# Last K/V chunk taken into the common loops of a one-core decode kernel, with a later wait in the loop and other small moves

## The chip, the cores and the metric

The kernel runs on one core of one Trainium2 chip. Times are microseconds (us) of device time for one execution. "us" in a result is the whole execution; the span of a trace, from first to last instruction, is some 2 us shorter. Engines: TensorE (PE in the profile; PEld is its weight load), VectorE (DVE), ScalarE (ACT), GpSimd (POOL), SyncE (SP). SP issues the large loads; "SPq" in a timeline is such an issue.

## The reference, cut to what matters

One query token, 16 query heads over 8 K/V heads, 65536 cached positions, head width 256, and a small MLP beside it. Nearly all the work is reading the caches once: 2 x 8 x 65536 x 256 bf16 values, 537 MB.

```python
q = (x @ wq).reshape(B, Sq, Hq, Dh).transpose(0, 2, 1, 3)
k, v = jnp.repeat(k_cache, 2, axis=1), jnp.repeat(v_cache, 2, axis=1)
scores = jnp.einsum("bhqd,bhkd->bhqk", q, k) * (Dh ** -0.5)
o = jnp.einsum("bhqk,bhkd->bhqd", softmax(scores), v)
a = o.transpose(0, 2, 1, 3).reshape(B, Sq, Hq * Dh) @ wo
b = token_mlp(layernorm(x), w1, b1, w2, b2)        # 448 x 1792, elementwise
return g * a + (1 - g) * b                         # g = sigmoid(sum(x * gate_w))
```

## The kernel before

Each K/V head's cache is cut into six chunks of 6, 6, 5, 5, 5 and 5 blocks of 2048 positions: 48 chunks in all. There are two K buffers and one V buffer, and three buffers `kT` for transposed blocks. SP issues the loads in one order, each behind a semaphore that VectorE raises:

```python
def load_k(i):                          # two K buffers
    if i >= 2: sp.wait_ge(s_vf, i - 1)
    sp.dma_start(out=kbuf[i % 2][:, 0:n], in_=kv_src(A_k_cache, i)).then_inc(s_k[i % 2], 16)
def load_v(i):                          # one V buffer
    if i >= 1: sp.wait_ge(s_vf, i + 1)  # s_vf: +1 for each drained P*V
    sp.dma_start(out=vbuf[:, 0:n], in_=kv_src(A_v_cache, i)).then_inc(s_v, 16)
# order on SP: wq (two loads), K0, K1, [projection done] V0, wo, K2, then V1, K3, V2, K4, ...
```

For each chunk VectorE transposes the K blocks into `kT`, TensorE scores each, and P·V of the chunk *before* is put between them:

```python
plan = [(0, 1), (1, 2), (2, 0), (3, 1), (5, 2), (4, 0)]   # (block, kT buffer)
def turns(i):                                             # VectorE
    take(dve, s_k[i % 2], 16)                             # K chunk landed
    for t, (s, b) in enumerate(blocks(i)):
        if t >= 3:                                        # its kT buffer must be free
            take(dve, s_s, 6 - steps[i] + 1 if t == steps[i] - 1 else 1)
        dve.transpose(out=kT[b], in_=kn[block s]).then_inc(s_kt, 1)
    # ... then, in the same chunk: wait for P*V of the chunk before, drain it (s_vf), wait for exp,
    #     transpose P for the next P*V
def scores(s, b, first, last):                            # TensorE: 8 matmuls on kT[b]
    ...
    if last:     ins.then_inc(s_sc, 1)
    elif s < 3:  ins.then_inc(s_s, 1)                     # blocks 0, 1, 2 free a kT buffer
```

On TensorE a loop ran 47 of the 48 turns: score blocks 0 to 3, P·V of the chunk before, the remaining score blocks. The 48th was written out after the loop: all five score blocks, then P·V of chunk 46, then the P·V of the last V, which arrives in four pieces, and the output projection.

The softmax here doesn't subtract the row's maximum and nothing guards it: scores larger than these inputs give would overflow.

## Time and profile before

| | before |
|---|---|
| median of four runs | 1266.46 us (1266.18 to 1266.92) |
| span of the trace | 1264.1 us |
| bytes read | 544.22 MB |
| busy PE / DVE | 57% / 53% |
| transfers, middle of the run | 433 GB/s |

The page of the kernel before: busy shares, then the share of the transfer engines and what they moved in 40 equal slices of 31.6 us.

```profile
PE 721.0 (57%) x4296; PEld 282.0 (22%) x4296; DVE 666.8 (53%) x471; ACT 50.1 (4%) x127; POOL 76.7 (6%) x98
...
DMA  9999999999999999999999999999999999999998
GB/s 407 424 439 430 437 438 425 438 434 428 440 437 423 434 436 433 440 430 435 434 429 435 430 435 440 430 429 437 430 440 435 430 431 435 427 443 435 424 435 350
```

No compute engine is near full; the transfers are, in every slice. The kernel is bound by bytes.

The start of the timeline before: start, duration, engine, line, operation, and in brackets the idle time before it.

```profile
31.50 13.28 DVE L528 STREAM_TRANSPOSE kT<-kbuf 128x2048 f32<-128x2048 f32 x6 [5.82 <-DVEq L520]
...
47.70 0.71 DVE L575 STREAM_TRANSPOSE pT<-p_t 128x512 bf16<-128x512 bf16 x1 [2.38 <-DVEq L520]
48.33 13.23 DVE L528 STREAM_TRANSPOSE kT<-kbuf 128x2048 f32<-128x2048 f32 x6
...
62.41 0.69 DVE L538 COPY og<-pv 128x512 f32<-128x512 f32 x1 [0.84 <-DVEq L520]
63.13 0.33 SPq L247 DMA_DIRECT2D vbuf<-in_A_v_cache_dram  x1
...
70.52 8.89 DVE L528 STREAM_TRANSPOSE kT<-kbuf 128x2048 f32<-128x2048 f32 x4 [3.11 <-DVEq L520]
```

VectorE begins its first transpose at 31.50 us, after 5.82 us of idle.

```profile
L241 SPq DMA_DIRECT2D kbuf<-in_A_k_cache_dram x1: 432/432/432, 1.9 to 1.9; - x1
...
DMA to landing us min/median/max: 25.0/25.0/25.0
```

In this document the time of that first transpose is called T0. The six transposes of chunks 0 and 1 run without a gap. After chunk 0 VectorE goes straight on to chunk 1, because K1 has already landed. At 62.41 the first P·V is drained and 0.72 us later SP issues the second V load (V1). At 70.52 VectorE takes up K2, the load that stands before V1 in the queue; it landed at 70.39.

The same stretch late in the run:

```profile
1201.46 0.69 DVE L539 TENSOR_TENSOR og<-pv,og 128x512 f32<-128x512 f32 x1 [1.86 <-DVEq L520]
1202.18 0.33 SPq L247 DMA_DIRECT2D vbuf<-in_A_v_cache_dram  x1
...
1211.07 2.31 DVE L528 STREAM_TRANSPOSE kT<-kbuf 128x2048 f32<-128x2048 f32 x1 [6.34 <-DVEq L520]
```

Here the V load is issued 8.9 us before the K load ahead of it lands.

And the tail before:

```profile
1247.83 1.91 PE L661 MATMUL sc<-kT,qw 128*128 128x512 bf16 x8 [0.87 <-PEq L657]
1249.66 2.33 PE L675 MATMUL pv<-vbuf,pT 128*4 128x512 bf16 x40
...
1253.32 1.25 PE L771 MATMUL pv<-kbuf,pT 128*4 128x512 bf16 x20 [0.17 <-DMA kbuf<-in_A_v_cache_dram]
...
1258.84 1.43 PE L782 MATMUL misc<-pT,kbuf 128*128 128x2 bf16 x48 [0.56 <-DMA kbuf<-in_A_v_cache_dram]
...
1261.11 0.28 DVE L823 CAST res<-acc 97x112 bf16<-97x112 f32 x1 [0.65 <-PE acc L816]
```

### The profile page before, as it was taken

The page shows a single profiled execution, that of the slowest core. Times are in us where ns is not written, and L with a number is a line of the kernel's source. Part 1 is how long each engine was busy: PE and PEld are TensorE (multiplying, and loading weights), DVE is VectorE, ACT ScalarE, POOL GpSimd, SP SyncE. Part 2 cuts the span into 40 slices and gives each one's busy share as a digit, 9 for nine tenths or more (in the row PEclk, how much of TensorE's full clock was granted, in tenths as well). Part 3 has the DMA queues.
Part 4 walks back from the last instruction along what each step waited for, and adds up shares of the span by engine and source line. Part 5 has one row for each costly group of instructions (what it writes and reads, how often), then busy time and mean ns, then how long its engine had stood idle before and what let it go on. Part 6 is the DMA issues. An engine that isn't in the chain of part 4 may idle for free. (4 is left out here: it accounts for less than half of the span.)

```text
span 1264.1 us, 10739 instructions
## 1 busy us (share of the span) xinstructions
PE 721.0 (57%) x4296; PEld 282.0 (22%) x4296; DVE 666.8 (53%) x471; ACT 50.1 (4%) x127; POOL 76.7 (6%) x98
## 2 busy tenths in 40 slices
PE   3755655456555665556554564566645755456556
PEld 1321222122221222212221221222212222122212
DVE  4845555365544645455555554465545654466444
ACT  0000000000000000000000000000000000000000
POOL 0001010110101101001011011000000000000000
PEclk9876788778777787777887788777877787778887
DMA  9999999999999999999999999999999999999998
GB/s 407 424 439 430 437 438 425 438 434 428 440 437 423 434 436 433 440 430 435 434 429 435 430 435 440 430 429 437 430 440 435 430 431 435 427 443 435 424 435 350
DMA packets 16842, 544.32 MB, mean 431 GB/s; under 512 B 1856, under 2 KB 3906, under 8 KB 4162
## 3 DMA queue, kind: packets, MB, share of 16 engines
q1 hardware_dynamic: 16744, 544.22, 99.7%
q8 instruction: 3, 0.05, 0.0%
q14 instruction: 5, 0.04, 0.0%
q10 hardware_dynamic: 90, 0.01, 0.0%
HBM read 544.22 MB, written 0.00 MB: 431 GB/s over the span
## 5 line engine op out<-in xcount | busy, mean ns | idle before, releaser
L661 PE MATMUL sc<-kT,qw 128*128 128x512 bf16 x2048 | 564.5, 438 | 458.6 <-PEq L657 458.6
L528 DVE STREAM_TRANSPOSE kT<-kbuf 128x2048 f32<-128x2048 f32 x256 | 571.1, 2283 | 310.7 <-DVEq L520 310.7
L661 PEld LDWEIGHTS sc<-kT,qw 128*128 128x128 bf16 x2048 | 213.7, 108 | 807.7 <-issue 644.1
L675 PE MATMUL pv<-vbuf,pT 128*4 128x512 bf16 x2008 | 130.5, 412 | 54.6 <-PEq L709 54.2
L539 DVE TENSOR_TENSOR og<-pv,og 128x512 f32<-128x512 f32 x39 | 27.0, 692 | 108.8 <-DVEq L520 106.3
L675 PEld LDWEIGHTS pv<-vbuf,pT 128*4 128x4 bf16 x2008 | 50.6, 92 | 132.4 <-issue 92.9
L608 ACT ACTIVATE p_t<-sc 128x512 bf16<-128x512 f32 x48 | 28.7, 597 | 1190.0 <-PE sc L661 1190.0
L585 DVE STREAM_TRANSPOSE pT<-p_t 128x512 bf16<-128x512 bf16 x32 | 22.8, 711 | 74.3 <-DVEq L520 74.3
L635 POOL TENSOR_SCALAR t_b<-t_b 128x448 f32<-128x448 f32 x14 | 7.9, 566 | 359.9 <-ACT t_b L617 359.9
L639 POOL TENSOR_SCALAR t_b<-t_b,hw 128x448 f32<-128x448 f32 x14 | 9.0, 640 | 333.4 <-ACT t_b L625 333.4
L538 DVE COPY og<-pv 128x512 f32<-128x512 f32 x8 | 5.5, 692 | 35.4 <-DVEq L520 35.4
L575 DVE STREAM_TRANSPOSE pT<-p_t 128x512 bf16<-128x512 bf16 x8 | 5.7, 711 | 26.9 <-DVEq L520 26.9
L644 POOL TENSOR_TENSOR ymix<-ymix,t_b 128x448 f32<-128x448 f32 x14 | 16.1, 1149 | 1.1
L643 POOL TENSOR_TENSOR t_b<-t_b,u_b 128x448 f32<-128x448 f32 x14 | 15.8, 1128 | 1.2
L638 POOL TENSOR_TENSOR t_b<-t_b,u_b 128x448 f32<-128x448 f32 x14 | 15.8, 1127 | 1.2
L731 PE MATMUL acc<-wo,oT 128*1 128x448 bf16 x28 | 7.0, 374 | 12.7 <-PEq L728 12.7
L591 DVE STREAM_TRANSPOSE pT<-p_t 128x512 bf16<-128x512 bf16 x7 | 5.0, 711 | 13.1 <-DVEq L520 13.1
L617 ACT ACTIVATE t_b<-h_bc,b1T,w1T 128x448 f32<-128x448 f32 x14 | 10.5, 747 | 0.0
L631 POOL TENSOR_SCALAR u_b<-h_bc,w1T,b1T 128x448 f32<-128x448 f32 x14 | 10.0, 718 | 4.1 <-DVE pat L430 2.7
L608 ACT ACTIVATION_READ_ACCUMULATOR p_t<-sc 128x1 f32 x48 | 9.3, 194 | 0.0
L685 PEld LDWEIGHTS misc<-mask,og 128*128 128x128 f32 x64 | 8.7, 196 | 2.3 <-DVE og L539 1.3
L448 PE MATMUL sc<-vbuf,xw 128*128 128x512 bf16 x32 | 9.0, 449 | 0.0
(89 smaller groups left out, 70.3 us busy)
## 6 DMA issues: line engine op xcount, KB each, us to landing
kbuf<-in_A_k_cache_dram SPq DMA_DIRECT2D x32, 5120.0 KB, 33.2
vbuf<-in_A_v_cache_dram SPq DMA_DIRECT2D x31, 5120.0 KB, 20.8
kbuf<-in_A_k_cache_dram SPq DMA_DIRECT2D x16, 6144.0 KB, 36.1
vbuf<-in_A_v_cache_dram SPq DMA_DIRECT2D x16, 6144.0 KB, 24.2
wo<-in_A_wo_dram SPq DMA_DIRECT2D x7, 448.0 KB, 22.3
vbuf<-in_A_wq_dram SPq DMA_DIRECT2D x1, 3072.0 KB, 10.2
kbuf<-in_A_v_cache_dram SPq DMA_DIRECT2D x1, 2560.0 KB, 26.5
kbuf<-in_A_v_cache_dram SPq DMA_DIRECT2D x1, 1280.0 KB, 31.1
```

Source lines behind the costliest of these rows:

```text
L448: last = e.matmul(q_ps[:], lhsT=xw[:, k, HKV - 1 - n:HKV - 1 - n + 128], rhs=rhs, start=(n == 0 and k == 0), stop=(n == HKV - 1 and k >= K ...
L528: dve.transpose(out=kT[b][:].bitcast(FP32), in_=kn[:, s * SB * 128:(s + 1) * SB * 128]).then_inc(s_kt, 1)
L539: return dve.tensor_tensor(out=og[:], in0=pv[:], in1=og[:], op=ALU.add)
L585: dve.transpose(out=pT_t[0][:], in_=p_t[:]).then_inc(s_pt, 1)
L608: ins = act.activation(out=p_t[:], in_=sc[:], func=ACT.Exp, scale=scale, accum_out=den[:, c:c + 1])
L617: ins = act.activation(out=t_b[:], in_=h_bc[:], func=ACT.Square, scale=w1T[:, b:b + 1], bias=b1T[:, b:b + 1],)
L631: lambda: pool.tensor_scalar(out=u_b[:], in0=h_bc[:], scalar1=w1T[:, b:b + 1], scalar2=b1T[:, b:b + 1], op0=ALU.mult, op1=ALU.add,),
L638: lambda: pool.tensor_tensor(out=t_b[:], in0=t_b[:], in1=u_b[:], op=ALU.mult),
L643: lambda: pool.tensor_tensor(out=t_b[:], in0=t_b[:], in1=u_b[:], op=ALU.mult),
L644: lambda: pool.tensor_tensor(out=ymix[:], in0=ymix[:], in1=t_b[:], op=ALU.add),
L661: ins = pe.matmul(sc[:], lhsT=qw[:, q, at:at + 128], rhs=kv[:, :, q // 2, :, q % 2], start=(first and q == 0), stop=(last and q == 7), ski ...
L675: ins = pe.matmul(pv[32 * a:32 * a + 4, :], lhsT=pT[:, k, :, ROW0 + s], rhs=vt[:, j * DH:(j + 2) * DH], start=first and k < 4, stop=last a ...
```

## The change

The intent is one loop for all 48 chunks on both engines, with fewer registers and semaphore steps, and a shorter prologue on VectorE. It has five parts:

1. TensorE and VectorE loops run 48 turns; the last P·V of chunk 46 now stands before the last score block; drains, den sums and the row matmuls of the tail move.
2. In the loop, score block 0 no longer raises the semaphore. The fourth transpose, which overwrites the buffer of block 0, now waits for score block **1**.
3. The small loads on the ACT queue are split by rows or parts: nine loads, not six.
4. The ten mask-row memsets and three other memsets go from VectorE to GpSimd.
5. The multiplies that write the next head's query columns (`queries`) go behind the den sums on VectorE.

```diff
@@ VectorE, turns(i)
-                if t >= 3:
-                    take(dve, s_s, 6 - steps[i] + 1 if t == steps[i] - 1 else 1)
+                if t in (3, steps[i] - 1):
+                    take(dve, s_s)
@@ TensorE, scores()
-            elif s < 3:
+            elif s in (1, 2):
                 ins.then_inc(s_s, 1)
@@ small loads
-        do.dma("act", x_row[:], A_x[0], writes=["x_row"])
-        do.dma("act", gw_row[:], gate_w.rearrange("(o n) -> o n", o=1), writes=["gw_row"])
-        for k, src in enumerate((B_w1[0, :], B_b1, B_w2[:, 0])):
-            do.dma("act", wrow[:, k, :], src.rearrange("(b p) -> b p", p=128), writes=[f"wrow{k}"])
+        for t, src, key, parts in ((x_row, A_x[0, 0], "x_row", 8), (gw_row, gate_w, "gw_row", 7)):
+            do.dma("act", t[...in parts], src[...in parts], writes=[key])        # cut
+        for k, (src, cut) in enumerate(((B_w1[0, :], 9), (B_b1, 2), (B_w2[:, 0], 3))):
+            for lo, hi in ((0, cut), (cut, NF)):
+                do.dma("act", wrow[lo:hi, k, :], src[128 * lo:128 * hi]..., writes=[f"wrow{k}{lo}"])
@@ TensorE loop
-        with nc.Fori(0, total - 1, 1, engines=[PE], head_slot={PE: 0}):
+        with nc.Fori(0, total, 1, engines=[PE], head_slot={PE: 0}):
             for s, b in plan[0:4]:
                 scores(s, b, s == 0, False)
-            with pe.If_lt(f_reg, 1):
+            with pe.If_lt(v_reg, PER):
                 ... P*V of the chunk before ...
             with pe.If_lt(c_reg, big):
                 scores(5, 2, False, False)
             scores(4, 0, False, True)
@@ after the loop
-        for t, (s, b) in enumerate(blocks(last_i)):
-            scores(s, b, t == 0, t == steps[-1] - 1)
-        ... P*V of chunk 46, den sums ...
+        # (both now in the loops; row matmuls moved behind the last V matmuls)
```

## The prediction

> **What bounds it now.** The transfers. The page's slices show DMA at 9 tenths in nearly all 40, and 423 to 443 GB/s in all but the first (407) and the last (350). 544.3 MB at the 433 to 434 GB/s of the middle windows take about 1255 us of the 1264.1 us span; the rest is the wait for first data and the tail. PE is busy 57%, DVE 53%. The Trainium skill ("DMA: Bandwidth & Descriptors", "Where 436 GB/s comes from") gives a ceiling of 435 GB/s; this trace agrees, so no instruction order can speed up the middle. The chain of waits has the last V load for 31.1 us, then 48 small PE matmuls (1.44 us), oT 0.17, output matmuls 0.57, cast 0.28.
>
> **Slack in the middle.** In the timeline a V load is issued at 1202.2 us, 0.7 us after its drain began; the K load queued before it lands only at 1211.1. So 9 us of transfers are still queued: compute that ends 1 or 2 us later empties nothing.
>
> **What the change does.**
> - Prologue: DVE loses the ten row memsets (1.24 us together) and three others (0.57); GpSimd gets them. ACT issues 9 small loads, not 6, at 0.2 to 0.5 us each. The one-element load landed at 10.9 us though issued at 3.0; with more pieces ahead it should land 1 to 4 us later, and the projection (12.9 to 21.7 us) with it. DVE idles 5.8 us until K lands at 31.5, and the first V is wanted only near 40 us. Absorbed.
> - Loop: the fourth transpose waits for the second score block, not the first. With TensorE at its low clock (430 ns a matmul, 3.4 us a block) it starts about 1.5 to 2 us later; scores, P·V and drain perhaps 1 us later. Absorbed by 9 us.
> - Last chunk: before, five score blocks (to 1249.7), then 40 P·V matmuls (2.33 us). After, P·V stands before the last score block (1.92 us), so the last transpose ends about 1253.3 to 1254, not 1251.3. The first piece of last V lands about 1253.3 and its 20 matmuls take 1.25 us; the next lands at 1255.7, the last at 1258.8. The lateness, under 1 us, is caught up there, as are one more drain (0.69) and the den sums (about 1 us).
> - True tail: the four row matmuls (0.37 us) now follow the last V matmuls, beside the oT multiply (0.24 us with its wait): +0.1 to +0.2 us.
>
> **Critical path.** Bytes, large loads and their order are unchanged. Sum: +0.2 us in the tail, 0 to 0.5 us if shadows are tighter than I read, minus at most 0.5 us if the small loads happen to even out the engines' finishing times.
>
> **Prediction:** 1266.8 us, 8 in 10 between 1265.4 and 1268.2. Faster by over 2%: 0.01; within 2%: 0.98; slower by over 2%: 0.01.
>
> **What would show it.** DMA 9 throughout, 544.3 MB; the chain again the last V piece, then the 48 matmuls; DVE busy about 1 us lower; GpSimd 1.5 to 2 us higher; a gap before the fourth transpose where there was none; P·V of the chunk before last ahead of the last score block; the last 20-matmul piece within 1 us of before.
>
> **What would make it wrong.** Loads issued so late that the queue runs dry at each chunk (48 times a microsecond would be 4%): windows with DMA below 0.97. A prologue late by over 9 us. The last V matmuls held by a late transpose (starting after 1259 us). A changed transfer rate from another cause, which the GB/s row would show.

## The result, and the profile after

Four runs took 1267.25 to 1269.83 us, median 1267.95, against 1266.46 before: 1.5 us or 0.1% longer, where 0.2 us had been forecast. The ratio to before is 1.0014, 95% interval 0.9996 to 1.0031. Ratios here are the mean time of one kernel's fast runs over that of the other's of the same rounds, so they are not quite the ratio of the medians quoted.

An interval that wide does not establish 0.1% alone. The traces do, because they show where the time went. The unchanged kernel has long executions too: 4 of its 29 runs took 1267.1 to 1267.95 us. Of the 21 runs of kernels with the later wait in the first two chunks, 19 took over 1267.

The page after, the same lines:

```profile
PE 719.3 (57%) x4296; PEld 276.0 (22%) x4296; DVE 675.2 (53%) x462; ACT 50.1 (4%) x127; POOL 78.7 (6%) x111
...
DMA  9999999999999999999999999999999999999998
GB/s 409 420 408 435 439 436 425 437 435 431 434 436 430 432 441 433 428 434 435 435 439 433 429 435 433 429 437 431 432 441 434 428 433 435 430 439 436 428 433 342
```

The DMA row is unchanged to the digit: a tenth is too coarse here. The GB/s row has one odd number, the third: 408, where before has 439. That slice is 63 to 95 us. The same place in short windows, first before, then after (columns: window, length, busy time and count of PE, PEld, DVE, ACT and POOL, granted clock, DMA share, GB/s; a packet counts whole in the window in which it starts, so a share can exceed 1):

```profile
63.00:66.00 3.00, 2.84 (x14) 1.06 (x11) 0.10 (x1) 0.13 (x1) 0.00 (x0) 1.00 1.01 437
66.00:69.00 3.00, 0.00 (x0) 0.00 (x0) 0.71 (x1) 0.56 (x2) 0.00 (x0) 0.82 1.10 475
69.00:72.00 3.00, 0.00 (x0) 0.00 (x0) 1.48 (x1) 0.00 (x0) 0.00 (x0) 0.50 1.06 459
```

```profile
63.00:66.00 3.00, 3.00 (x32) 1.23 (x36) 3.00 (x2) 0.00 (x0) 0.00 (x0) 1.00 1.01 437
66.00:69.00 3.00, 3.00 (x39) 1.18 (x28) 1.90 (x2) 0.00 (x0) 0.00 (x0) 1.00 0.57 246
69.00:72.00 3.00, 2.15 (x10) 0.77 (x8) 0.00 (x0) 0.69 (x2) 0.00 (x0) 1.00 1.13 377
```

From 66 to 69 us the transfer engines are busy 57%. Summing the packets of the trace from 66 to 80 us gives 6.07 MB before and 5.25 MB after. The 0.82 MB missing are 1.9 us at 433.9 GB/s, the mean of before in that stretch. I call such a loss, counted from 66 to 80 us, the *dip* below. From 100 to 1200 us both traces average 433.5 GB/s: nothing is lost there and nothing won back. The two spans differ by 2.5 us. With each packet spread over its duration, the trace after is 0.04 us of bytes behind at 66 us, 1.94 at 80 us and 1.96 at 1250 us: all of the lost bytes lie in those 14 us. The rest comes at the very end, where the last piece of V lands 1.7 us after the piece before it (below).

The timeline after, for the same events as shown of before:

```profile
33.40 6.70 DVE L539 STREAM_TRANSPOSE kT<-kbuf 128x2048 f32<-128x2048 f32 x3 [6.28 <-DVEq L531]
...
41.26 6.70 DVE L539 STREAM_TRANSPOSE kT<-kbuf 128x2048 f32<-128x2048 f32 x3 [1.16 <-DVEq L531]
...
51.52 6.66 DVE L539 STREAM_TRANSPOSE kT<-kbuf 128x2048 f32<-128x2048 f32 x3
...
60.50 6.70 DVE L539 STREAM_TRANSPOSE kT<-kbuf 128x2048 f32<-128x2048 f32 x3 [2.33 <-DVEq L531]
...
67.72 0.69 DVE L549 COPY og<-pv 128x512 f32<-128x512 f32 x1 [0.52 <-DVEq L531]
68.44 0.33 SPq L248 DMA_DIRECT2D vbuf<-in_A_v_cache_dram  x1
...
72.66 6.66 DVE L539 STREAM_TRANSPOSE kT<-kbuf 128x2048 f32<-128x2048 f32 x3
```

The six transposes have fallen into three and three, with a gap before the fourth: 1.16 us in chunk 0, 2.33 us in chunk 1. V1 is issued at 68.44 us, 5.3 us later than before. Of that, 1.9 us were already there at T0 (33.40 against 31.50, though K0 had landed at 27.1 us), and 3.4 us come from the two chunks: from T0 to V1 it takes 35.0 us, not 31.6. At 72.66 VectorE no longer waits for K2.

The tail after:

```profile
1249.74 2.33 PE L682 MATMUL pv<-vbuf,pT 128*4 128x512 bf16 x40
1252.01 1.92 PE L668 MATMUL sc<-kT,qw 128*128 128x512 bf16 x8
...
1255.66 1.25 PE L747 MATMUL pv<-kbuf,pT 128*4 128x512 bf16 x20 [0.89 <-PEq L531]
...
1260.51 1.21 PE L758 MATMUL misc<-pT,kbuf 128*128 128x2 bf16 x40 [0.56 <-DMA kbuf<-in_A_v_cache_dram]
...
1262.24 0.37 PE L758 MATMUL misc<-pT,kbuf 128*128 128x2 bf16 x8 [0.53 <-DMA kbuf<-in_A_v_cache_dram]
...
1263.64 0.28 DVE L813 CAST res<-acc 97x112 bf16<-97x112 f32 x1 [0.82 <-PE acc L806]
```

P·V of chunk 46 now stands before the last score block. The 20 matmuls on the first piece of the last V start 0.7 us after it landed (1254.94), but at the next pieces PE is idle and waiting when they land, so the new order is in the shadow of that load, as in the kernel before.

### The profile page after: what moved, and what is told of

The parts are those of the page before. It is cut to its first block, busy times and chain, and to the rows that moved or that the text cites. A ratio compares the mean times of both kernels' runs of the same rounds, so it can differ in the third digit from the quotient of the medians.

```text
span 1266.6 us, 10628 instructions
## 1 busy us (share of the span) xinstructions
PE 719.3 (57%) x4296; PEld 276.0 (22%) x4296; DVE 675.2 (53%) x462; ACT 50.1 (4%) x127; POOL 78.7 (6%) x111
## 5 line engine op out<-in xcount | busy, mean ns | idle before, releaser
L668 PE MATMUL sc<-kT,qw 128*128 128x512 bf16 x2048 | 571.4, 437 | 490.2 <-PEq L664 490.2
L668 PEld LDWEIGHTS sc<-kT,qw 128*128 128x128 bf16 x2048 | 210.7, 108 | 849.9 <-issue 696.4
L682 PE MATMUL pv<-vbuf,pT 128*4 128x512 bf16 x2008 | 119.9, 387 | 26.0 <-PEq L712 25.9
L682 PEld LDWEIGHTS pv<-vbuf,pT 128*4 128x4 bf16 x2008 | 47.0, 88 | 95.9 <-issue 50.0
L586 DVE STREAM_TRANSPOSE pT<-p_t 128x512 bf16<-128x512 bf16 x8 | 5.7, 711 | 26.9 <-DVEq L531 26.9
## 6 DMA issues: line engine op xcount, KB each, us to landing
kbuf<-in_A_v_cache_dram SPq DMA_DIRECT2D x1, 2560.0 KB, 25.6
```

Of the source, the lines that this page charges most:

```text
L668: ins = pe.matmul(sc[:], lhsT=qw[:, q, at:at + 128], rhs=kv[:, :, q // 2, :, q % 2], start=(first and q == 0), stop=(last and q == 7), ski ...
L682: ins = pe.matmul(pv[32 * a:32 * a + 4, :], lhsT=pT[:, k, :, ROW0 + s], rhs=vt[:, j * DH:(j + 2) * DH], start=first and k < 4, stop=last a ...
```

## The experiments

Theory A: the later wait of the fourth transpose delays the first drain so far that the queue runs dry before V1 is issued. Theory B: the split small loads make one transfer engine late, and with it the first K chunk and the end. Theory C: the tail, or chance. Rival D: the later wait costs a little at every chunk. The edits are named by what they undo in the diff above. Where an expectation says that the first K lands, read T0.

The traces of e5 to e8 that are kept are of other executions than those described under e5 to e8, whose packets can't be summed again.

### e1: the later wait undone

```diff
  (changed kernel)
-                if t in (3, steps[i] - 1): take(dve, s_s)
+                if t >= 3: take(dve, s_s, 6 - steps[i] + 1 if t == steps[i] - 1 else 1)
-            elif s in (1, 2):
+            elif s < 3:
```

> The changed kernel with one thing undone: the fourth transpose waits for the first score block again, as before. Theory A (the second V load is issued too late and the transfer queue runs dry at 66 to 72 us): the second V load, issued at 68.4 us in the changed kernel and at 63.1 before, comes back to about 65.0 (3.4 us earlier: 1.3 from chunk 0 and 2.1 from chunk 1); the GB/s of 66 to 69 us goes from 246 to above 420; the time falls by 1.3 to 1.9 us against the changed kernel, to a ratio of 1.0000 to 1.0003 to before. Theory B (the split small loads make one transfer engine late, and it stays late to the end): nothing is gained at the end, the ratio stays 1.001 to 1.0015. Theory C (the tail, or chance): also 1.001 to 1.0015, with the dip filled and another loss in its place or none.

Measured: 1266.05 us (1265.95 to 1267.47, five runs), ratio 0.9997 (0.9983 to 1.0010). T0 was 33.39, V1 came at 65.92 us, the dip was 0.61 us. Its window of 66 to 72 us:

```profile
66.00:72.00 6.00, 2.63 (x13) 0.96 (x10) 2.19 (x2) 0.69 (x2) 0.00 (x0) 0.95 0.99 393
```

The loss is gone from the time though the small loads stay split and T0 is late: against B and C. The GB/s did not come back as fully as expected, because V1 was 0.9 us later than I had forecast; the clock, taken up after the table, accounts for that.

### e2: the old small loads

```diff
  (changed kernel)
-  nine split loads on ACT
+  the six loads of before
```

> The changed kernel with the six small loads of before (six, not nine, on ACT). Theory A: the first K chunk lands at 31.5 us again instead of 33.4, so the second V load is issued about 66.5 us, just where the queue ends: most of the dip is gone, ratio 1.0001 to 1.0006. Theory B: the late engine is gone, ratio about 1.0000 to 1.0003, and the last two pieces of V land within 0.5 us of each other (1.7 us apart in the changed kernel). If the first K chunk still lands after 33 us, the small loads did not make it late.

Measured: 1268.34 us (1266.89 to 1268.73), ratio 1.0008 (0.9995 to 1.0022). T0 was 33.53 us all the same, V1 came at 68.63, dip 2.09 us. A miss for what I expected under A, whose numbers rested on T0 coming back to 31.5; and B fails here, since without the split loads T0 is late and the loss is whole.

### e3: both undone

```diff
  (changed kernel)
   the edits of e1 and of e2 together
```

> The changed kernel with both the early wait of the fourth transpose and the small loads of before: only the merged loops, the moved tail and the mask rows on GpSimd are left. Theories A and B: as before within 0.3 us, ratio 0.9997 to 1.0003, second V load at 63 to 63.5 us. Theory C (the tail costs it): ratio 1.0005 to 1.0015.

Measured: 1266.18 us (1266.12 to 1266.35), ratio 0.9996 (0.9982 to 1.0009). T0 31.55, V1 at 64.69 (later than expected), dip 0.02 us. Its last V landed at 1258.88 us, within 0.04 of before, and the final cast began 0.21 us later than before (1261.32 against 1261.11). That is the tail's cost: about 0.2 us, against C. The merged loops and the mask rows on GpSimd cost nothing that can be seen in the time.

### e4: only the later wait, in the kernel before

```diff
  (kernel before)
-                if t >= 3: take(dve, s_s, 6 - steps[i] + 1 if t == steps[i] - 1 else 1)
+                if t in (3, steps[i] - 1): take(dve, s_s)
-            elif s < 3:
+            elif s in (1, 2):
```

> The kernel before with only the later wait of the fourth transpose added. Theory A: second V load at about 66.5 us (63.1 plus 3.4), at the end of the queue; a small dip in the GB/s of 66 to 69 us; ratio 1.0000 to 1.0005. If the wait costs at every chunk (a rival that the windows of the changed kernel speak against), the ratio is above 1.001.

Measured: 1268.42 us (1267.96 to 1269.01), ratio 1.0014 (1.0001 to 1.0028): the whole loss, from this part alone, in the kernel before. T0 33.19, V1 at 67.83, dip 1.42 us:

```profile
66.00:72.00 6.00, 4.54 (x36) 1.66 (x26) 1.87 (x3) 0.69 (x2) 0.00 (x0) 1.00 0.99 369
```

The size is above my figure for A. By that expectation it would have spoken for D, so D had to be tested by itself.

### e7 and e8: the later wait by chunk

Both start from e1, where TensorE raises the semaphore three times in each chunk. The wait is later only where `late` holds:

```diff
-                if t >= 3: take(dve, s_s, 6 - steps[i] + 1 if t == steps[i] - 1 else 1)
+                late = i >= 2          # e7;  e8: i < 2   (i: chunk within the group of six)
+                if t >= 3:
+                    if late:
+                        if t == 3: take(dve, s_s, 2)
+                        elif t == steps[i] - 1: take(dve, s_s)
+                    else: take(dve, s_s, 6 - steps[i] + 1 if t == steps[i] - 1 else 1)
```

> The changed kernel, but in the first two chunks of each group of six the fourth transpose waits for the first score block only (as before); in the other four chunks, 32 of the 48, it keeps the later wait. Theory A (only the first drain has no queue behind it, so only the delay of chunks 0 and 1 costs): second V load at 64.7 to 66 us, no 246 in the GB/s row of 66 to 69 us, time as the run with the early wait everywhere, 1266.0 to 1266.5, ratio 0.9995 to 1.0003. Rival D (the later wait costs a little at every chunk): two thirds of the loss stays, ratio 1.0008 to 1.0012.

> The opposite: the later wait only in the first two chunks of each group of six, the early one in the other 32. Theory A: the whole loss, 1267.3 to 1268.5, ratio 1.0008 to 1.0016, dip of the GB/s at 66 to 72 us. Rival D: a third of the loss, ratio 1.0003 to 1.0006, no dip.

Measured, e7: 1266.46 us (1265.83 to 1267.88), ratio 1.0002 (0.9988 to 1.0015), V1 at 65.12, dip 0.11. e8: 1268.60 us (1266.68 to 1268.71), ratio 1.0011 (0.9997 to 1.0024), V1 at 68.10, dip 1.58. First e7, then e8:

```profile
66.00:72.00 6.00, 1.83 (x9) 0.60 (x7) 2.08 (x2) 0.69 (x2) 0.00 (x0) 0.82 1.02 434
```

```profile
66.00:72.00 6.00, 4.81 (x40) 1.81 (x32) 1.87 (x3) 0.69 (x2) 0.00 (x0) 1.00 0.92 344
```

Thirty-two late waits cost nothing; the sixteen others, of which two lie before V1, cost all of it. D would have it the other way round. The ratios alone overlap; the dip and the medians do not. The kept trace of e7 is one of its long executions (span 1266.9 us, V1 at 66.15, dip 1.11), though its chunks 0 and 1 run without a gap; the clock was late there (below). It speaks no more for D: its bytes are 1.16 us behind those of before at 80 us and 1.15 at 1200.

### e5 and e6: the small loads by themselves

e5 is the kernel before with the nine split loads of the change (its diff above). e6 is the kernel before with six more one-row loads on ACT:

```diff
         do.dma("act", b2_row[:], ...)
+        for n in range(6):
+            do.dma("act", spare[:, n, :], B_b1[128 * n:128 * n + 128]..., writes=[f"spare{n}"])
```

> The kernel before with nothing but the nine split small loads. After the run with the old loads put back (first K landed at 33.5 us there too) I expect them to cost nothing: first V late by about 1 us, first K at 31.5 or about 33.4 us by chance, second V at 63 to 66 us, time as before, ratio 0.9997 to 1.0004. Theory B (split loads make one engine late): first K after 33 us and ratio above 1.0008.

> The kernel before with six more one-row loads on the ACT queue into a tile nobody reads. Theory B': every small load adds a fixed delay to one and the same engine, so the first K chunk, which needs all sixteen, lands 2 us later or more (after 33.5 us), and the second V load moves with it. Chance: first K at 31.5 or about 33.4 us as in the runs so far, ratio 0.9997 to 1.0005.

Measured, e5: 1266.77 us (1266.21 to 1267.92), ratio 1.0004 (0.9990 to 1.0017), T0 33.52, V1 at 65.87, dip 0.69. e6: 1266.42 us (1266.31 to 1267.61), ratio 1.0001 (0.9986 to 1.0017), T0 31.60, V1 at 63.20, no dip. The Trainium skill ("DMA: Bandwidth & Descriptors", "Why a DMA increments its semaphore by 16 and not by 1") says that a load which uses fewer than sixteen transfer engines goes to the lowest-numbered of them. That was the ground of theory B. The trace does not name the engine of a packet, but in all eighteen kept traces, with split, old or added loads, K0 itself landed at 26.6 to 27.2 us: no small load made it late, and B' is refuted.

### e9 to e12: where the two times of T0 come from

e9: kernel before, only the three row loads split. e10: kernel before, only the two one-row loads split. e11: kernel before, unchanged. e12: e5 again.

```diff
  e9 (kernel before)
-        for k, src in enumerate((B_w1[0, :], B_b1, B_w2[:, 0])): one load each
+        for k, (src, cut) in enumerate(((B_w1[0, :], 9), (B_b1, 2), (B_w2[:, 0], 3))): two loads each
  e10 (kernel before)
-        do.dma("act", x_row[:], ...); do.dma("act", gw_row[:], ...)
+        the same two loads, written as 8 and 7 parts
```

> The kernel before with only the three row loads split (six loads, 9 and 5, 2 and 12, 3 and 11 rows). So far the first K chunk landed late (33.4 to 33.5 us) in 5 of 5 traces with the nine split loads and in 2 of 5 without them. If the split of the rows is the cause: after 33.3 us. If chance: 31.5 or 33.4. Time as before within 0.1%.

> The kernel before with only the two one-row loads split in 8 and 7 parts. If spreading these is the cause of the late first K: after 33.3 us; if the rows are, or chance: 31.5 at least as often. Time as before within 0.1%.

> The kernel before, unchanged, for one more trace. If the landing of the first K is chance: 31.5 or 33.4 us, with the second V load at 63.1 or 65.0 us, and in the second case still no more than 0.2 us lost at 66 to 72 us.

> The kernel before with the nine split loads, once more. If these make the first K late: after 33.3 us a sixth time. If chance: 31.5 us is as likely.

Measured, with two runs each: e9 1267.17 us, T0 33.32, V1 64.96, dip 0.05. e10 1267.24 us, T0 33.42, V1 66.68, dip 1.13. e11 1266.27 us, T0 33.37, V1 64.77, dip 0.00. e12 1266.19 us, T0 33.12, V1 64.70, dip 0.01. The unchanged kernel can have its T0 late too, and pays nothing for it: V1 is still in time. e10 has the early wait and a dip all the same: there the two chunks took 33.3 us from T0 to V1, not 31.4 as in e11. The windows of chunk 1 show the granted clock (the number before the last two) lower for longer, first e10, then e11:

```profile
54.00:57.00 3.00, 3.00 (x8) 1.04 (x7) 3.00 (x2) 0.00 (x0) 0.00 (x0) 0.50 0.89 366
57.00:60.00 3.00, 3.00 (x11) 1.20 (x10) 2.94 (x3) 0.00 (x0) 0.00 (x0) 0.70 1.04 448
```

```profile
54.00:57.00 3.00, 3.00 (x12) 1.13 (x11) 3.00 (x3) 0.00 (x0) 0.00 (x0) 0.74 0.89 366
57.00:60.00 3.00, 3.00 (x16) 1.31 (x14) 3.00 (x2) 0.00 (x0) 0.00 (x0) 1.00 1.04 448
```

The first 32 score matmuls of chunk 1 took 9.82 us in e10 and 8.57 in e11, and P·V and the drain came later with them.

### e13 to e16: one trace more of four kernels

e13: the changed kernel. e14: e2. e15: the kernel before. e16: e5.

> The changed kernel once more, one trace. Dose: whatever the landing of the first K chunk L is (31.5 or 33.4 us so far), the second V load comes at L plus 35.0 us, and what the queue loses at 66 to 76 us is about 0.57 us for each us after 65.0: about 0.9 us for L = 31.5, about 1.9 us for L = 33.4.

> The changed kernel with the old small loads, once more. So far the old loads had the first K at 31.5 in 3 of 6 traces and at 33.2 to 33.5 in the other 3; loads with a split had it at 33.1 to 33.5 in 8 of 8. Chance with the old loads: either. Dose as for the changed kernel.

> The kernel before, once more: first K at 31.5 or 33.4 us; second V load 31.5 us after it; loss at 66 to 76 us under 0.1 us either way.

> The kernel before with the split loads, once more: first K after 33 us again if the split makes it late, 31.5 possible if it is chance. Second V load 31.5 to 32.5 us after it; loss under 0.7 us.

Measured (single runs): e13 1268.50 us, T0 33.47, V1 67.92, dip 1.54. e14 1268.28 us, T0 33.33, V1 68.45, dip 1.94. e15 1266.30 us, T0 31.50, V1 63.13, dip 0.00. e16 1266.17 us, T0 33.16, V1 64.79, dip 0.01. e13 tested the dose. V1 came 0.5 us earlier than the expected 35.0 us after T0; for that V1, 0.57 us per us after 65.0 gives 1.66, near the 1.54 measured.

### All traces in one table

Ordered by the issue of V1. The dip is from the packet sums; the GB/s are those of 66 to 72 us; us is the profiled run.

| trace | wait of 4th transpose | small loads | T0 | V1 issued | dip, us | GB/s | us |
|---|---|---|---|---|---|---|---|
| before | early | old | 31.50 | 63.13 | 0.00 | 467 | 1266.30 |
| e15 | early | old | 31.50 | 63.13 | 0.00 | 442 | 1266.30 |
| e6 | early | old + 6 | 31.60 | 63.20 | 0.00 | 459 | 1266.48 |
| e3 | early | old | 31.55 | 64.69 | 0.02 | 475 | 1266.13 |
| e12 | early | split | 33.12 | 64.70 | 0.01 | 475 | 1265.96 |
| e11 | early | old | 33.37 | 64.77 | 0.00 | 467 | 1266.33 |
| e16 | early | split | 33.16 | 64.79 | 0.01 | 457 | 1266.17 |
| e9 | early | rows split | 33.32 | 64.96 | 0.05 | 467 | 1266.35 |
| e7 | early in chunks 0, 1 | split | 33.49 | 65.12 | 0.11 | 434 | 1266.21 |
| e5 | early | split | 33.52 | 65.87 | 0.69 | 377 | 1266.77 |
| e1 | early | split | 33.39 | 65.92 | 0.61 | 393 | 1266.71 |
| e10 | early | x split | 33.42 | 66.68 | 1.13 | 385 | 1268.17 |
| e4 | late | old | 33.19 | 67.83 | 1.42 | 369 | 1268.30 |
| e13 | late | split | 33.47 | 67.92 | 1.54 | 352 | 1268.50 |
| e8 | late in chunks 0, 1 | split | 33.47 | 68.10 | 1.58 | 344 | 1268.60 |
| after | late | split | 33.40 | 68.44 | 1.90 | 311 | 1268.43 |
| e14 | late | old | 33.33 | 68.45 | 1.94 | 287 | 1268.28 |
| e2 | late | old | 33.53 | 68.63 | 2.09 | 279 | 1268.73 |

Up to 65.0 us at most 0.05 us is lost; after that about 0.55 us for each us. Every trace of the table lies within about 0.2 us of this line, whichever edit made V1 late. The six traces with the late wait in chunks 0 and 1 need 34.5 to 35.1 us from T0 to V1, the twelve others 31.4 to 33.3. The kept traces of e5 to e8 have T0 33.45, 33.42, 33.76 and 33.32, V1 at 65.08, 64.82, 66.15 and 68.32, and dips of 0.33, 0.00, 1.11 and 2.05 us: up to 0.5 us above the line.

The dip is a mean over the sixteen transfer engines, and the span can grow by more. In e10 and in the kept trace of e7 two or three engines stand idle for about 2 us after 68 us while the rest work on; the dips are 1.1 us, the spans 1.9 and 2.8 us longer than that of before.

**The clock.** In the kept traces with the early wait in chunks 0 and 1, V1 comes 31.4 to 31.6 us after T0 where the full clock of chunk 1 is granted 22.1 to 23.5 us after T0 (eight traces), and 32.4 to 33.3 us where it is granted 24.2 to 25.4 us after it (e1, e3, e7, e10). This delay, of up to 1.9 us, does not come from the later wait, which these chunks don't have. With a late T0 it goes with a dip, as in e10. It may be what makes some executions of the unchanged kernel long; that is not shown, as none of those has a trace.

**What ends the idle before T0.** The same in all eighteen kept traces: VectorE executes a branch that ends at 25.6 to 27.9 us, then nothing, not even a register instruction (the trace has these, the views leave them out), until 0.2 us before T0, though K0 lands at 26.6 to 27.2. Among the packets in between is one of the kind "instruction", of 8 KB. It starts at 29.5 us where the branch ended by 26.0 (before, e3, e15), and at 31.1 to 31.7 us where it ended at 26.5 or later (the fifteen others); T0 follows its start by 2.0 to 2.1 us each time. My reading is that VectorE stands still for its next instructions, whose fetch waits among the large loads; this is argued, not tested, as the trace doesn't name the engine that a fetch is for. The two times of T0 go with how early the projection is done. In all 22 traces T0 is 31.5 to 31.6 where V0 was issued by 22.01 us, and 33.1 to 33.8 where it was issued at 22.41 or later.

The experiments point to no version that beats both: e1, e3 and e7 are all the same as before within their intervals. With the queue full the bytes set the time.

## Why the prediction was right or wrong, point by point

- **Bound by bytes, middle unaffected: right.** 433.5 GB/s from 100 to 1200 us in both traces. The Trainium skill's ceiling of 435 GB/s ("DMA: Bandwidth & Descriptors", "Where 436 GB/s comes from") agrees with it.
- **"Absorbed by 9 us" (the loop): wrong, and this is the step that failed.** It had three errors, all in one direction.
  1. The slack was read late in the run (8.9 us) and taken for the whole. At V1 the same reading of the kernel before gives 70.52 - 63.13 = 7.4 us.
  2. The landing of the load ahead is not the moment at which the queue runs dry. The table shows the loss starting at 65.0 us, 5.5 us before that landing. Part of this shows in the packets of the trace after: fourteen of the sixteen engines are done with K2 at 67.9 to 69.0 us, up to 2.5 us before it has landed whole, and V1's first packet starts 0.96 us after its issue. The other 2 us or so are not explained. So 1.9 us were usable before V1, not 9.
  3. The delay was set at "perhaps 1 us". In the steady state that is about the size, since each chunk waits for its own K (5.3 us of idle before it in the trace after at 1212 us) and the delay of one chunk does not reach the next. In chunks 0 and 1 it adds up: K1 has already landed when chunk 0 ends, so 1.16 and 2.33 us make 3.5. To this came a T0 that was 1.9 us later.
- **The sum: 0.2 us forecast, 1.5 us measured.** The missing term is the dip, 1.9 us in the trace after (1.5 in its second trace), which the forecast had as 0. It did name the mechanism among what would make it wrong, a queue that runs dry, but looked for it at every chunk rather than once.
- **The fourth transpose starts later: right**, with its reason. The Trainium skill ("TensorE: Matmul & The Clock Gate", "Part 1: The HAM clock gate") says that TensorE's clock is halved after an idle stretch. The trace agrees: weight loads of the first scores of chunk 0 stand 0.43 us apart, and a warm block of eight matmuls takes 1.90 us, 0.24 us each. Two cold blocks would take about 6.9 us, and the first begins only when the first transpose is done, 2.4 us in; three transposes take 6.70 us. So a wait for the second block bites exactly here. The gap was 1.16 us and not 2.6 in chunk 0, because the clock was granted in full from about 39.1 us on.
- **Prologue "absorbed": wrong, by a misread wait.** The one-element load was used at 11.76, not 10.86 us, and V0 was issued at 23.3, not 21.9. The prediction gave this the 5.8 us for which VectorE idles "until K lands at 31.5". K0 had landed at 26.9, and the lateness was not absorbed: T0 came 1.9 us later. Alone it costs next to nothing (e9, e11, e12 and e16 lose at most 0.05 us); with the later wait it adds to the same V1.
- **Last chunk in the shadow, +0.1 to +0.2 in the tail: right.** e3, which has this tail and a full queue, casts 0.2 us later than before.
- **DVE busy about 1 us lower: wrong.** It is 8.4 us higher (675.2 against 666.8), and 674.1 in e3 too, whose time is that of before: without effect on the time. The group means show part of it: the query multiply rose from 408 to 561 ns a piece, the add of the den sum to `og` from 678 to 824. **GpSimd 1.5 to 2 us higher: right** (76.7 to 78.7).
- **"The chain again the last V piece, then the 48 matmuls": in part.** It ends in the last V piece, but this landed 1.7 us after the piece before it, so only 8 matmuls were left. The 20 matmuls of the first piece start 2.3 us later than before (1255.66 against 1253.32), not within 1 us.

**What stays open.** With the small loads of before T0 was early in 4 of 8 traces of the table, with any split in 0 of 10. If the split had no influence, all four early ones would fall among the eight by chance with a probability of 0.023 (70 of 3060 ways). So the split probably makes the projection late, and with it T0; but the projection is late at times with the old loads too (e2, e4, e11, e14). No trace has the late wait together with an early T0, so it is not known how much of the dip an early T0 would have spared. With the early wait in chunks 0 and 1, the table's five traces with a late T0 and 31.4 to 31.7 us from it to V1 lose at most 0.11 us, the kept one of e5 loses 0.33.

## What to carry to other kernels

In a kernel bound by transfers, ask of each wait how late it makes the *issue* of the next load, and measure the slack at the place where least is queued ahead of it, which is often the first reuse of a buffer and not the steady state. Delays are forgotten at each chunk while compute waits for data, but add up where data is already there. Read the slack as the time until bandwidth falls, not until the load ahead has landed; here the difference was 5.5 us of an apparent 7.4. And before idle time is counted as slack, check in the trace that it ended with the event that you suppose: VectorE's idle before T0 outlasted the landing of K0 by 4.6 us.

## What the Trainium skill lacked or had wrong

- "DMA: Bandwidth & Descriptors" ("Anatomy of one DMA") says that transfer engines do not wait on semaphores, only the issuing sequencer does. The trace agrees: V1 was issued 0.72 us after the start of its drain in both kernels. I did not find there how far ahead of an emptying queue the next load must be issued: here bandwidth was lost as soon as it was issued less than 5.5 us before the landing of the load ahead, at about 0.55 us per us.
- The same page, "Where 436 GB/s comes from", says that for transfers between HBM and SBUF the HBM side (about 358) binds. With one core running, 433.5 GB/s were read from HBM here for 1100 us. "HBM Reference", "Specifications (TRN2)", has it nearer, with about 425 for a core streaming alone.
